# Attention, routing and gated layers on one Trainium2 core: a split, rows, squares, the logits' turn and the constants of attention in other places of the order

## Chip, cores and metric

The kernel runs on one core of a Trainium2 chip, in one launch. The metric is the device time of one execution in microseconds (us). One execution is profiled: its span, from its first to its last instruction, and the waits inside it are read from its trace. TensorE is PE in the rows (PEld its weight loads), VectorE is DVE, ScalarE is ACT, GpSimd is POOL and SyncE is SP.

## The reference

Three stages follow each other. The attention has no sum over a row: a sigmoid stands where a softmax would.

```python
scores = scale * np.matmul(q, k.transpose(0, 1, 3, 2)) - np.log(S)   # 4 x 12 heads, S = 448, width 64
attn = 1.0 / (1.0 + np.exp(-scores))
x = np.matmul(attn, v)                                               # -> 1792 tokens x 768

xn = x / (np.linalg.norm(x, axis=-1, keepdims=True) + 1e-06)         # experts' directions alike: en
logits = xn @ en.T / tau                                             # 8 experts
expert_idx = np.argmax(logits, axis=1)
out[mask] = gate_w[mask, None] * (np.maximum(x[mask] @ w1[e], 0.0) @ w2[e])   # F = 1024

gate = 1.0 / (1.0 + np.exp(-(x @ w_gate)))                           # x: the 1792 x 768 of the experts
return (gate * (x @ w_val)) @ w_out                                  # F = 1536
```

## The kernel before

**Exact products from two parts.** Nearly every matrix product is computed as three: an operand is split into a rounded part `hi` and the rest `lo`, and hi*hi, hi*lo and lo*hi are added in PSUM. For weights, `split_next` takes the next chunk of 128 x 1536 from the list `order`: ACT casts it to `hi` (L213), VectorE subtracts (L214). A parameter `hi_eng` lets VectorE do the cast too. The two parts go into a ring of four buffers, and `take` hands them out in the same order. `split_pair` does the same for queries and keys of a pair of heads, both steps on VectorE (L351, L352).

**Attention.** It handles the heads in pairs, 24 in all, six for each of four sequences, and one turn of the loop `for g in range(2 * ND + 1)` works on one pair, g = 0 to 24. In a turn TensorE computes scores in units of 128 keys (`qk_unit`, L377), ACT applies the sigmoid (L379), and later TensorE multiplies with the values (`av_unit`, L391). All `av` products of the kernel share one PSUM tile of two halves, one for each pair of two. When a pair's last unit is added, VectorE copies its half out as `xT` (L396), and TensorE begins the other pair's next products only after that copy. Two pairs share one unit of left-over keys, which runs as unit 3.

**What is hung into the turns.** The function `attention_hooks(g, pos)` is called three times a turn: pos 0 at its start, pos 1 behind the scores, pos 2 behind the value products. Everything else is written out there by hand, so the place in this function is the place in each engine's order: splits of the next pair, loads, the decoding of 64-bit weights on VectorE (L196, L199, L202), `logits` (L407, TensorE, added up in `lgT` on VectorE, L411 and L413), `logits_turn` (L417, one transpose of `lgT` on TensorE, then a copy, L418), `rows_unit`, and from `G0 = 19` on the first steps of the routing. With the loop's turn counted from G0, `at_` (3, 2), (4, 0) and (4, 2) are the places of the first three weight splits.

**Rows and squares.** `rows_unit(b, c)` turns 112 tokens of a finished sequence from columns to rows: six transposes on TensorE (L431), a copy on ACT (L433), a store to `xd` in memory that GpSimd issues (L434), and `square` on ACT (L423), which adds up the squares for the norm. The four parts of a sequence b have their places at turns `LG[b]`, +1, +2 and +2, all at pos 2, LG = 7, 13, 19. For the last sequence `rows_part` (L446, L448, L449) and `rows_pair` (L461, L464, L465) do it in pieces, and nine of their squares are kept in the list `squares` for later. The row copies share three buffers in SBUF (tag `xr`), so a copy waits until the store that used its buffer three copies before has landed.

**Constants and directions.** `prepare_constants` (L313 to L317 on VectorE, the square of the experts' directions on ACT, L321, its root on GpSimd, L323) and `prepare_directions` (L303 to L330, VectorE) make the normalized directions; `prepare_experts` turns them on TensorE (L334) and copies them to `en` on VectorE (L335).

**Behind attention.** `front(p)` gathers nothing itself: it transposes the gathered tokens of tile p (L839), casts them to `xh` (L844, ACT) and `xl` (L846, VectorE). `h_chunk(0, 0..3)` multiplies tile 0 with the four chunks of its expert's first weights (L990). In between stand the rest of the counting: `count`, `ranks`, `columns`, `first_ids` (L588, with a copy of the numbers to VectorE, L589), then `gather(1)` (L830), which GpSimd issues when these numbers and all stored rows are there. `place_a` to `place_c` work out on VectorE where each token goes, GpSimd multiplies (L595) and TensorE collects the ids (`psid`, L602).

**PSUM.** Beside the tile of `av` three slots of two banks go round: the fourth tile asked for waits until the first was read. A tile is read by ACT or VectorE, so TensorE waits for these engines in the order in which the slots go round.

Of the kernel before, what the change touches and what calls it, by code (L numbers as in the profile page):

```python
# [28 lines left out]
NCH = S // CP  # L29
# [18 lines left out]
NW1 = KD * F1 // CH  # L48
# [57 lines left out]
def routed_kernel(ctx: ExitStack, tc: tile.TileContext, kqP, vP, emb, tau, w1P, w2P, wffP, cst, out):  # L106
# [11 lines left out]
    def slot(name):  # L118
        return psp.tile([P, 2, 512], F32, tag="ps", name=name)
# [67 lines left out]
    def decode_load(k, src, dst):  # L187

        SP.dma_start(src.bitcast(U32), wffP[k].bitcast(U32))
        dec_t[k] = (src.bitcast(U32).rearrange("p (f w) -> p f w", w=2), dst)  # L190
# [19 lines left out]
    def split(raw, pool, name, width=CH, hi_eng=None):  # L210
        hi = pool.tile([P, width], F32R, tag="hi", name=f"hi{name}")[:, : raw.shape[1]]
        lo = pool.tile([P, width], F32R, tag="lo", name=f"lo{name}")[:, : raw.shape[1]]
        (hi_eng.tensor_copy if hi_eng else A.copy)(hi, raw)  # L213
        V.tensor_sub(lo, raw, hi)  # L214
        return hi, lo

    def split_next(ahead=None, hi_eng=None):
        i = done_split[0]
        if i >= len(order):
            return  # L220
        done_split[0] += 1
        parts[i] = split(raws[raw_of[i]], ring, i, hi_eng=hi_eng)
        j = next((j for j in range(i + 1, len(order)) if order[j][:2] == ("gv", 0) and order[j][2] in direct), None)
        if j == i + 1:
            f = order[j][2]
            for step in range(3):
                decode(f, step)
            if f + 2 in direct:
                decode_load(f + 2, stage64[f % 2], raws[raw_of[j + 2]])
        it = order[i]  # L230
        if i not in nxt:
            return
        free = [i]
        if it[0] in ("w1", "w2") and PA <= it[1] < PA + NA:

            free = [i - 1, i] if it[2] % 2 else []
            for z in free:
                (h_small if it[0] == "w1" else y_small)(it[1] - PA, order[z][2], raws[raw_of[z]])
        for z in free:
            if ahead is None:  # L240
                load(nxt[z])
            else:
                ahead.append(nxt[z])
# [3 lines left out]
    def take():  # L247
        i = used[0]
        used[0] += 1
        return parts.pop(i)  # L250
# [80 lines left out]
    def prepare_experts():  # L331
        pe_ = slot("pe_")
        for c in range(KD):
            T.transpose(pe_[:, 0, c * E : (c + 1) * E], emb_sb[:, c * P : (c + 1) * P], ident[:E, :E])  # L334
        V.tensor_copy(en[:, :, :E], pe_[:, 0, : KD * E].rearrange("p (c e) -> p c e", e=E))  # L335
        G.tensor_copy(ie[:, :P], ident)
        G.tensor_copy(ie[:, P:], en[:, KD - 1, :E])
# [3 lines left out]
    ss = cpool.tile([CP, NT], F32, name="ss")  # L341
# [79 lines left out]
    def square(xf, acc, name):  # L421
        junk = ap1.tile([CP, D], BF16, tag="junk", name=f"junk{name}")
        A.activation(junk[:, : xf.shape[1]], xf, AF.Square, accum_out=acc)  # L423

    def rows_unit(b, c):

        t = b * NCH + c
        ps = slot(f"xr{t}")
        pv = ps[:CP].rearrange("p a b -> p (a b)")[:, :D]
        for k in range(NPR):  # L430
            T.transpose(pv[:, k * P : (k + 1) * P], xT[b * NPR + k][:, c * CP : (c + 1) * CP], ident)  # L431
        x = ap2.tile([CP, D], F32, tag="xr", name=f"xr_sb{t}", bufs=3)
        A.copy(x, pv)  # L433
        G.dma_start(xd[t * CP : (t + 1) * CP, :], x)  # L434
        square(x, ss[:, t : t + 1], t)

    squares = []

# [94 lines left out]
    def columns(t0, t1):  # L533
        ts_ = slice(t0, t1)
        n = t1 - t0
        TT(out=bm[:, ts_], in0=bct(iota_h[:CP], n), in1=bc3(bi[:, ts_], P), op=ALU.is_equal)
# [48 lines left out]
    def first_ids(k, nt):  # L585
        ps = slot(f"ps0_{k}")
        for t in range(nt):
            T.matmul(ps[:, 0, 0:1], bm[:, t, :], am1[:, k, t : t + 1], start=(t == 0), stop=(t == nt - 1))  # L588
        V.tensor_copy(idx01[:, k : k + 1], ps[:, 0, 0:1])  # L589
# [278 lines left out]
        load_pair(n)  # L868

    ahead = []  # L870
    later = []
    ND = NP // 2

    LG = [NPR * (b + 1) + 1 for b in range(B - 1)]
    G0 = LG[-1]

    def attention_hooks(g, pos):

        at_ = (g - G0, pos)
        n = g + 1  # L880
        if pos == 0 and n < NP:
            split_pair(n)
        if pos == 1 and g % 2 == 0:
            for n in (g + 4, g + 5):
                if n < NP:
                    load_pair(n)
        if pos == 2 and (g + 1) // 2 < ND and g:
            load_v((g + 1) // 2, 1 - g % 2)
        for k in range(DEC_ATT):
            if (g, pos) == (2 * k + 1, 0):  # L890
                decode_load(DEC_ORDER[k], stage_att[k % 2], rawb[:, 2 + k % 2, :])
            for step, when in enumerate(((2 * k + 2, 1), (2 * k + 2, 2), (2 * k + 3, 1))):
                if (g, pos) == when:
                    decode(DEC_ORDER[k], step)
        if pos == 2 and g >= 3 and g % 2:
            logits([g - 3, g - 2])
        if (g, pos) == (1, 1):
            prepare_constants()
        elif (g, pos) == (1, 2):
            prepare_directions()  # L900
        elif (g, pos) == (2, 1):
            prepare_experts()
        for b in range(B - 1):
            if (g, pos) == (LG[b], 2):
                logits_turn(b)
                if b == B - 2:
                    choose(0, TE)
                    RED(out=ohf, in_=oh[:, :TE].rearrange("p t e -> p e t"), axis=AX.X, op=ALU.add)
                    V.tensor_copy(ohs, ohf)
                    V.tensor_copy(oh4, bct(ohf, NCH))  # L910
            for c in range(NCH):
                if (g - LG[b], pos) == ((0, 2), (1, 2), (2, 2), (2, 2))[c]:
                    rows_unit(b, c)
        if at_ == (1, 1):
            count(0, TE)
        elif at_ == (1, 2):
            fullest()
            expert[0] = SP.value_load(es["tile"], min_val=0, max_val=E - 1)
            ranks(0, TE)
            fullest_ids(0, TE)  # L920
            first_tiles(0, TE)
        elif at_ == (2, 1):
            columns(0, TE // 2)
        elif at_ == (2, 2):
            columns(TE // 2, TE)
        elif at_ == (3, 1):
            first_ids(0, TE)
            gather(0)
        for c, when in enumerate(((2, 1), (2, 2), (3, 1), (3, 2))):
            if at_ == when:  # L930
                load(order.index(("w1", 0, c)))
        if at_ == (4, 1):
            for k in (0, 1):
                load(order.index(("w2", 0, k)))
        for c, when in enumerate(((4, 1), (4, 2), (4, 2), (5, 1))):
            if at_ == when:
                rows_part(c)
        if at_ in ((3, 2), (4, 0), (4, 2)):
            split_next(ahead, hi_eng=V if at_ == (4, 0) else None)

    for g in range(2 * ND + 1):
# [36 lines left out]
    def h_chunk(p, c, between=None, part=None):  # L978
        if c == 0:
            hp_t[p] = slot(f"h{p}")  # L980
        ps = hp_t[p]
        xh, xl = xg_t["T", p]
        hi, lo = part or take()

        passes = ((xh, hi), (xh, lo), (xl, hi))
        for part in (passes[:2], passes[2:]) if c == 0 else (passes,):
            for s in range(3):
                k, half = divmod(3 * c + s, 2)
                for x, w in part:
                    T.matmul(ps[:, half, :], x[:, k * P : (k + 1) * P], w[:, s * 512 : (s + 1) * 512],  # L990
                             start=(k == 0 and x is xh and w is hi), stop=(k == KD - 1 and x is xl))
                if between and s == 1 - c and part[0][0] is xh:
                    between()
        if c == NW1 - 1:
            h = mp.tile([P, F1], F32, tag="h", name=f"hr{p}", bufs=1)
            h_t[p] = h
            relu(p)
# [224 lines left out]
    rows_pair(NPR - 1, SP)  # L1222
    choose(TE, NT)
    later.pop()()
    w1_0 = [take() for _ in range(NW1 - 1)]
    h_chunk(0, 0, lambda: count(TE, NT), part=w1_0[0])
    fullest_ids(TE, NT)
    for f in squares:
# [1 line left out]
    ranks(TE, NT)  # L1230
    first_tiles(TE, NT, (1,))
    columns(TE, NT)
    h_chunk(0, 1, lambda: first_ids(1, NT), part=w1_0[1])
    at.close()
    yTp = ctx.enter_context(tc.tile_pool(name="yT", bufs=1, reuse_waits="tile"))
# [6 lines left out]
    for k in range(2, NW2):  # L1242
        load(order.index(("w2", 0, k)))
    split_next(ahead)
    w1_0.append(take())
    h_chunk(0, 2, part=w1_0[2])
    h_chunk(0, 3, part=w1_0[3])
    place_a()
# [211 lines left out]
```

## Time and profile before

| | |
|---|---|
| median of 3 runs | 1015.85 us (1015.69 to 1016.33) |
| the profiled execution, its own time | 1015.3 us |
| its span | 1013.5 us |
| TensorE busy | 983.5 us, 97% |
| weight loads busy | 812.6 us, 80% |
| VectorE busy | 581.7 us, 57% |
| ACT busy | 485.3 us, 48% |
| GpSimd busy | 104.7 us, 10% |
| memory read, written | 197.46 MB, 31.16 MB |

The median is 0.55 us above the profiled execution, and 1.8 us of that execution's time lie outside of its span. Busy shares are means over stages of different kinds: attention fills about the first 160 us, the first tiles' routing the next 40, then come the experts and the gated layers. A row of a timeline gives the start in the span, the duration, and in brackets how long the engine stood idle before it and which instruction ended that. In the kernel's engines instructions run in the order in which they are written, so an instruction that waits holds up all behind it on its engine.

### The profile page before, as it was taken

The numbers are of one execution on the slowest core, as the hardware profiler recorded it, in microseconds if no ns is written. First come the engines' busy times: TensorE is split into PE (matmuls) and PEld (weight loads), VectorE is DVE, ScalarE is ACT, GpSimd is POOL, SyncE is SP. The second block draws the span as 40 slices with busy tenths as digits, with TensorE's granted clock in tenths as the row PEclk, the third lists the DMA queues.
The fourth block names the chain that finished last, engine by engine and source line by source line (L and its number), as shares of the span: only waits on it lengthen the run. The fifth ranks groups of instructions, "written<-read, shape, count | busy, mean of one in ns | idle before, by whom it ended". The sixth has DMA issues, their size and how long they took to land.

```text
span 1013.5 us, 15157 instructions
## 1 busy us (share of the span) xinstructions
PE 983.5 (97%) x6096; PEld 812.6 (80%) x6096; DVE 581.7 (57%) x652; ACT 485.3 (48%) x528; POOL 104.7 (10%) x103
## 2 busy tenths in 40 slices
PE   8999998989999999999999999999999999999995
PEld 4455454778888888889888899888899888999995
DVE  5867664987887777876588533333333333323551
ACT  5576675467776677776322422333322333223540
POOL 0011002213231221201000001000001000001001
PEclk9999998999999999999999999999999999999998
DMA  8999866374799974692578533322333322324530
GB/s 283 332 337 321 286 212 222 113 263 160 281 362 346 318 286 168 220 326 81 220 230 299 187 125 126 124 94 94 125 125 140 109 94 94 125 94 173 193 103 31
DMA packets 39695, 198.23 MB, mean 196 GB/s; under 512 B 5032, under 2 KB 7096, under 8 KB 37184
## 3 DMA queue, kind: packets, MB, share of 16 engines
q1 hardware_dynamic: 31584, 158.68, 45.5%
q0 software_dynamic: 8032, 38.51, 9.8%
q8 instruction: 49, 0.80, 0.3%
q14 instruction: 30, 0.25, 0.1%
HBM read 197.46 MB, written 31.16 MB: 226 GB/s over the span
## 4 chain that ended last, share of the span: by engine, by line
PE 73%; DMA 2%; issue 1%; DVE 0%; POOLq 0%
PE gv L1208 11%; PE gv L1209 11%; PE gv L1210 11%; PE h L990 7%; PE o L975 6%; PE o L976 6%; PE o L974 6%; PE y L974 3%; PE y L975 3%; PE y L976 3%; PE qh L1079 2%; PE qy L1102 1%; PE hTp L1009 1%; DMA xg<-xd,idx 1%; PE yTp L1194 1%
## 5 line engine op out<-in xcount | busy, mean ns | idle before, releaser
L214 DVE TENSOR_TENSOR lo<-rawb,hi 128x1536 fp32r<-128x1536 f32 x176 | 307.2, 1758 | 295.8 <-ACT hi L213 293.1
L213 ACT CAST hi<-rawb 128x1536 fp32r<-128x1536 f32 x175 | 258.1, 1480 | 240.7 <-PE gv L1209 97.2
L1208 PE MATMUL gv<-yT,hi 128*128 128x512 f32 (+1 forms) x576 | 208.9, 363 | 0.0
L1210 PE MATMUL gv<-yT,lo 128*128 128x512 f32 (+1 forms) x576 | 208.9, 363 | 0.0
L1209 PE MATMUL gv<-yT,hi 128*128 128x512 f32 (+1 forms) x576 | 208.8, 363 | 0.0
L1210 PEld LDWEIGHTS gv<-yT,lo 128*128 128x128 f32 x576 | 108.7, 189 | 16.9
L1208 PEld LDWEIGHTS gv<-yT,hi 128*128 128x128 f32 x576 | 108.7, 189 | 16.7
L1209 PEld LDWEIGHTS gv<-yT,hi 128*128 128x128 f32 x576 | 108.7, 189 | 16.6
L974 PE MATMUL o<-hi,gh 128*128 128x384 f32 x336 | 112.8, 336 | 0.0
L976 PE MATMUL o<-lo,gh 128*128 128x384 f32 x336 | 112.3, 334 | 0.0
L975 PE MATMUL o<-hi,gl 128*128 128x384 f32 x336 | 112.3, 334 | 0.0
L379 ACT ACTIVATE attn<-sc,bias_s 128x896 f32<-128x896 f32 x84 | 78.3, 1005 | 30.4 <-PE sc L377 30.4
L1368 ACT CAST gh<-sg 128x512 fp32r<-128x512 f32 (+1 forms) x48 | 27.2, 567 | 129.8 <-DVE sg L1367 129.8
L391 PE MATMUL av<-attn,v 128*64 128x448 f32 (+1 forms) x384 | 72.9, 558 | 6.1 <-DVE xT L396 6.1
L974 PE MATMUL y<-hi,hh 128*128 128x384 f32 x208 | 72.1, 346 | 0.0
L990 PE MATMUL h<-hi,xh 128*128 128x512 f32 x168 | 68.3, 406 | 3.6 <-PEq L1133 3.5
L975 PE MATMUL y<-hi,hl 128*128 128x384 f32 x208 | 70.1, 337 | 0.0
L976 PE MATMUL y<-lo,hh 128*128 128x384 f32 x208 | 70.0, 336 | 0.0
L990 PE MATMUL h<-lo,xh 128*128 128x512 f32 x168 | 66.3, 395 | 0.1
L975 PEld LDWEIGHTS o<-hi,gl 128*128 128x128 f32 x336 | 63.1, 188 | 0.1
L974 PEld LDWEIGHTS o<-hi,gh 128*128 128x128 f32 x336 | 63.1, 188 | 0.1
L976 PEld LDWEIGHTS o<-lo,gh 128*128 128x128 f32 x336 | 63.1, 188 | 0.0
(304 smaller groups left out, 1178.0 us busy)
## 6 DMA issues: line engine op xcount, KB each, us to landing
rawb<-wd SPq DMA_DIRECT2D x65, 768.0 KB
rawb<-in_w1P SPq DMA_DIRECT2D x52, 768.0 KB
rawb<-in_w2P SPq DMA_DIRECT2D x52, 768.0 KB
rawb<-in_wffP SPq DMA_DIRECT2D x16, 1536.0 KB
wd<-rawb POOLq DMA_DIRECT2D x16, 768.0 KB, 6.7
kq<-in_kqP SPq DMA_DIRECT2D x24, 448.0 KB
xd<-xr_sb POOLq DMA_DIRECT2D x12, 336.0 KB, 7.3
y<-yd SPq DMA_DIRECT2D x10, 384.0 KB
```

The lines of the kernel that those rows point to most:

```text
L213: (hi_eng.tensor_copy if hi_eng else A.copy)(hi, raw)
L214: V.tensor_sub(lo, raw, hi)
L379: A.activation(at_, ps[:, :, :S], AF.Sigmoid, bias=bias_s, scale=1.0 / math.sqrt(HD))
L391: T.matmul(av_t[j * HD : (j + 1) * HD, i % 2, :S], v[rows, j * HD : (j + 1) * HD], at_[rows, j, :], start=(u == first_unit(i)), stop=(u == ...
L974: T.matmul(o, ah[:, ks], bh[:, w], start=(k == 0), stop=False)
L975: T.matmul(o, al[:, ks], bh[:, w], start=False, stop=False)
L976: T.matmul(o, ah[:, ks], bl[:, w], start=False, stop=(k == nk - 1))
L990: T.matmul(ps[:, half, :], x[:, k * P : (k + 1) * P], w[:, s * 512 : (s + 1) * 512], start=(k == 0 and x is xh and w is hi), stop=(k == KD ...
L1208: T.matmul(o, hi[:, a, k, :], yh[:, k, :n], start=(k == 0), stop=False)
L1209: T.matmul(o, hi[:, a, k, :], yl[:, k, :n], start=False, stop=False)
L1210: T.matmul(o, lo[:, a, k, :], yh[:, k, :n], start=False, stop=(k == KD - 1))
L1368: A.copy(gh[:, f, :n], sg[:, :n])
```

## The change

No instruction is added or removed: the engines have as many rows as before, in another order. Five things move. `prepare_constants` goes from the hook (1, 1) to (0, 1) and `prepare_directions` from (1, 2) to (1, 1). In a turn of `LG`, `rows_unit` now comes ahead of `logits_turn`. The squares of a sequence's third and fourth rows (c = 2, 3) are put off to the next pos 1, behind four sigmoids. The third weight split leaves (4, 2), in the last full turn, and comes behind `columns(TE, NT)`, between the first two chunks of tile 0. As its parts are taken later, `take` is called for two chunks first and for two later on.

```diff
-    def rows_unit(b, c):
+    def rows_unit(b, c, put_off=None):
...
-        square(x, ss[:, t : t + 1], t)
+        if put_off is None:
+            square(x, ss[:, t : t + 1], t)
+        else:
+            put_off.append(lambda: square(x, ss[:, t : t + 1], t))
...
-    later = []
+    later, put_off = [], []
...
-        if (g, pos) == (1, 1):
+        if (g, pos) == (0, 1):
             prepare_constants()
-        elif (g, pos) == (1, 2):
+        elif (g, pos) == (1, 1):
             prepare_directions()
         elif (g, pos) == (2, 1):
             prepare_experts()
+        if pos == 1:
+            while put_off:
+                put_off.pop(0)()
         for b in range(B - 1):
+            for c in range(NCH):
+                if (g - LG[b], pos) == ((0, 2), (1, 2), (2, 2), (2, 2))[c]:
+                    rows_unit(b, c, put_off if c > 1 else None)
             if (g, pos) == (LG[b], 2):
                 logits_turn(b)
...
-            for c in range(NCH):
-                if (g - LG[b], pos) == ((0, 2), (1, 2), (2, 2), (2, 2))[c]:
-                    rows_unit(b, c)
...
-        if at_ in ((3, 2), (4, 0), (4, 2)):
+        if at_ in ((3, 2), (4, 0)):
             split_next(ahead, hi_eng=V if at_ == (4, 0) else None)
...
-    w1_0 = [take() for _ in range(NW1 - 1)]
+    w1_0 = [take() for _ in range(NW1 - 2)]
...
     columns(TE, NT)
+    split_next(ahead)
     h_chunk(0, 1, lambda: first_ids(1, NT), part=w1_0[1])
...
     split_next(ahead)
-    w1_0.append(take())
+    w1_0 += [take(), take()]
     h_chunk(0, 2, part=w1_0[2])
```

TensorE at the first logits' turn (g = 7, pos 2; `lp` are the logits, `lg` the turned logits, `xr` the rows). Before:

```order
L407 MATMUL lp_632<-xT_545,en 32x112 x4
L407 MATMUL lp_632<-xT_585,en 32x112 x4
L417 MATMUL lg_642<-cs,lgT_416 112x128
L431 MATMUL xr_645<-cs,xT_310 112x128
L431 MATMUL xr_645<-cs,xT_360 112x128
```

and now:

```order
L407 MATMUL lp_632<-xT_545,en 32x112 x4
L407 MATMUL lp_632<-xT_585,en 32x112 x4
L431 MATMUL xr_642<-cs,xT_310 112x128
L431 MATMUL xr_642<-cs,xT_360 112x128
L431 MATMUL xr_642<-cs,xT_433 112x128
L431 MATMUL xr_642<-cs,xT_473 112x128
L431 MATMUL xr_642<-cs,xT_545 112x128
L431 MATMUL xr_642<-cs,xT_585 112x128
L417 MATMUL lg_654<-cs,lgT_416 112x128
```

The six transposes of the rows have changed places with the one of the logits.

VectorE at the end of attention (the last two copies of `xT` are those of pairs 22 and 23). Before:

```order
L413 TENSOR_TENSOR lgT_1607<-lgT_1607,lp_1760 128x112
L214 TENSOR_TENSOR lo_1791<-rawb,hi_1790 128x1536
L396 COPY xT_1798<-av 128x448
L396 COPY xT_1814<-av 128x448
L413 TENSOR_TENSOR lgT_1607<-lgT_1607,lp_1816 128x112
```

and now:

```order
L413 TENSOR_TENSOR lgT_1607<-lgT_1607,lp_1760 128x112
L396 COPY xT_1794<-av 128x448
L396 COPY xT_1810<-av 128x448
L413 TENSOR_TENSOR lgT_1607<-lgT_1607,lp_1812 128x112
L418 COPY lg<-lg_1836 112x32
```

The `lo` of the third split is gone from here. It stands further on, as the next place shows for its `hi`.

ACT behind attention, now (`junk` are the squares that had been kept, nine in all, of which the last five are shown; before, only the second of the two casts stood here):

```order
L423 ACTIVATE junkp_3_1892,ssp<-xrp_sb 112x128
L423 ACTIVATE junkp_0_1894,ssp<-xrp_sb 112x128
L423 ACTIVATE junkp_1_1896,ssp<-xrp_sb 112x128
L423 ACTIVATE junkp_2_1898,ssp<-xrp_sb 112x128
L423 ACTIVATE junkp_3_1900,ssp<-xrp_sb 112x128
L213 CAST hi_1909<-rawb 128x1536
L213 CAST hi_1961<-rawb 128x1536
L1008 ACTIVATE hr_1983<-h_1859 128x512 x2
```

The cast of the third split (`hi_1909`) now waits behind the nine squares, next to that of the fourth. On VectorE its `lo` stands ahead of the copy of the numbers for `gather(1)`.

## Rows read from the trace of the kernel before

**Rows 1.** Waits of TensorE over the span: us in total, times, longest.

```profile
PE av L391 <- DVE xT L396: 6.1, 2, 4.4
...
PE lg L417 <- DVE lgT L413: 3.1, 3, 1.1
PE sc L377 <- ACT attn L379: 2.0, 3, 0.7
```

**Rows 2.** Page, part 2: busy share of the DMA engines, 40 slices, tenths.

```profile
DMA  8999866374799974692578533322333322324530
```

**Rows 3.** Timeline, VectorE and TensorE, 10 to 23 us: start, us, idle before.

```profile
10.85 0.63 DVE L351 CAST kqhi<-kq 128x896 fp32r<-128x896 f32 x1 [3.29 <-DMA kq<-in_kqP]
...
12.52 0.16 DVE L313 RECIPROCAL tau_sb<-tau_sb 128x1 f32<-128x1 f32 x1
...
14.53 0.14 DVE L303 TENSOR_SCALAR rt<-rt 8x1 f32<-8x1 f32 x1 [1.38 <-POOL rt L323]
...
19.07 2.48 PE L391 MATMUL av<-attn,v 128*64 128x448 f32 x12 [1.65 <-DVE xT L396]
...
20.48 0.20 DVE L335 COPY en<-pe__344 128x48 f32<-128x48 f32 x1
...
22.18 0.37 PE L377 MATMUL sc<-kqhi 64*128 64x448 f32 x2
```

**Rows 4.** Timeline, TensorE and VectorE, around the first and third logits' turn.

```profile
49.62 0.29 PE L417 MATMUL lg<-cs,lgT 128*112 128x128 f32 x1 [1.05 <-DVE lgT L413]
49.75 0.82 PE L431 MATMUL xr<-cs,xT 128*112 128x128 f32 x6
...
130.44 0.62 DVE L396 COPY xT<-av 128x448 f32<-128x448 f32 x1
...
131.54 2.48 PE L391 MATMUL av<-attn,v 128*64 128x448 f32 x12
```

**Rows 5.** Timeline, ACT and TensorE, around the first and third pair of rows.

```profile
67.62 0.47 PE L377 MATMUL sc<-kqhi 64*128 64x448 f32 x2 [0.66 <-ACT attn L379]
...
148.29 1.48 ACT L213 CAST hi<-rawb 128x1536 fp32r<-128x1536 f32 x1
...
150.38 2.80 ACT L379 ACTIVATE attn<-sc,bias_s 128x896 f32<-128x896 f32 x3 [0.60 <-PE sc L377]
...
151.49 0.65 PE L446 MATMUL xr<-cs,xT 128*112 128x128 f32 x4
```

**Rows 6.** Timeline, all engines, from the end of attention to tile 1.

```profile
153.95 0.55 POOL L449 DMA_DIRECT2D xd<-xr_sb  x1 [0.30 <-ACT xr_sb L448]
...
161.99 4.75 PE L391 MATMUL av<-attn,v 128*64 128x448 f32 x12 [4.41 <-DVE xT L396]
...
162.37 0.58 ACT L448 COPY xr_sb<-xr 112x512 f32<-112x512 f32 x1 [2.76 <-DMA xd<-xr_sb]
...
167.99 0.82 PE L839 MATMUL xTp<-cs,xg 128*128 128x128 f32 x6
...
169.85 0.48 PE L990 MATMUL h<-hi,xh 128*128 128x512 f32 x1
...
174.71 1.01 POOL L830 DMA_INDIRECT xg<-xd,idx  x1 [4.89 <-DVE idx L589]
...
174.76 1.47 ACT L213 CAST hi<-rawb 128x1536 fp32r<-128x1536 f32 x1
...
175.80 0.39 PE L990 MATMUL h<-lo,xh 128*128 128x512 f32 x1
...
176.26 1.76 DVE L214 TENSOR_TENSOR lo<-rawb,hi 128x1536 fp32r<-128x1536 f32 x1 [1.83 <-ACT hi L213]
...
180.04 0.82 PE L839 MATMUL xTp<-cs,xg 128*128 128x128 f32 x6
...
191.94 0.55 PE L602 MATMUL psid<-spi,bm 112*128 112x26 f16 x16 [1.10 <-POOL spi L595]
```

**Rows 7.** Windows, same place: length, busy of PE, PEld, DVE, ACT, POOL, clock, DMA.

```profile
162.00:164.00 2.00, 2.00 (x6) 0.76 (x8) 0.00 (x0) 0.58 (x1) 0.52 (x1) 0.50 0.03 12
```

## The prediction

> **What bounds the kernel now.** I read the list of TensorE's waits first, then the timeline around each, then the clock. TensorE is busy 97% of the span, so whatever moves the end is one of its few waits or its clock; VectorE and ACT, busy about half the time, matter only where TensorE waits for them. Three waits of the list lie in the stretch that the change touches [rows 1]: the value products for the copy `xT` (6.1 us in two places), the logits' turn for `lgT` (3.1 in three), the scores for a sigmoid (2.0 in three); 11.2 us together. [...] All later stages follow TensorE's order and shift as a whole, so what TensorE gains up to tile 1 (180 us) I carry to the end. Nothing is added: each gain below is a wait that goes, less the part that something later in line keeps.
>
> **A, constants and directions.** VectorE waited 3.29 us for the keys at the start, until 10.85 [rows 3]. The five constants (L313 to L317) now lie ahead of that wait and fit into it, if their loads are there. The directions then begin where the constants stood, at 12.52 and not at 14.53, 2.0 sooner, and with them the wait of 1.38 for the root from GpSimd is over, since ACT's square of the directions moves forward too. Everything behind on VectorE, the `xT` copy among it, comes 2.0 sooner. TensorE waited 1.65 for that copy before 19.07 [rows 3], so this wait goes whole. What is late next is `en`: its copy ran from 20.48 to 20.68, behind the decoding of weights that come by DMA and do not come sooner, and the score product that needs its PSUM slot, at 22.18 before, would be due at 20.53. I take 0.2 off: A = 1.4. Lower bound 1.1, if the constants' loads land with the keys (five small instructions of some 0.14, 0.16 by the first one's row, then cost 0.7 of the 2.0, and 0.2 stays lost); upper bound 1.65.
>
> **B, the logits' turn.** Three times TensorE stood 1.05 us before the turn, for an addition on VectorE that the change does not move [rows 1, 4]. Six transposes of rows, 0.82 us [rows 4], now run ahead of it. I count 0.75 of them, since the end of a product overlaps the next (the turn's own product runs 0.29, and the next starts 0.13 behind it). So 0.3 of each wait stays, and three times 0.75 = 2.25 goes. The third time something else is late: VectorE has the sequence's choice of experts to do, its `xT` copy ended at 130.44 + 0.62 = 131.06, and TensorE, which began the next value products at 131.54 [rows 4], would now arrive at 130.79. 0.3 is lost there: B = 1.95. Lower bound 1.5 (the third gives nothing), upper bound all 3.15.
>
> **C, the squares.** At the first two places the sigmoid that TensorE waits 0.66 for [rows 5] stands behind two squares. A row copy of 112x512 takes 0.58 on ACT [rows 6]; by that a square of 112x768 is estimated at 0.87, and two put off free 1.7, more than the wait: 1.3 for both. The third time the squares come ahead of the cast `hi` at 148.29 [rows 5]. The cast starts some 0.45 later, and so does the sigmoid behind it, which waited 0.60 for its scores; the wait of 0.67 goes, but the transposes of the last sequence's rows, at 151.49, wait for the slot which that sigmoid reads, and get 0.2 of it. C = 1.5, between 1.2 (the third turns to a loss of 0.1) and 2.0.
>
> **D, the third split.** VectorE's `lo` (1.76 us) and the wait for its `hi` stood ahead of the last `xT` copies. Without them the value products start at 161.99 - 4.41 = 157.6, and without that idle time I expect full clock: 2.48 and not 4.75, another 2.3. TensorE would then be free for tile 0's transposes (167.99 [rows 6]) at about 161.4, 6.6 sooner. But these need the slot which ACT's last row copy reads, and that copy waited until 162.37 for a store that GpSimd issued at 153.95, three copies earlier [rows 6]. Nothing moves the store. The copy ends at 162.95, the transposes start at 163.0, and the first chunk's products (169.85) at 164.9: 5.0 sooner, not 6.6.
>
> What is late next is the split itself. ACT has nine squares and then a cast; that cast began at 174.76 with no idle time before it [rows 6], so now at 169.8. It ends at 171.2 (1.47), VectorE's `lo` (1.76) at 173.0. The third chunk's second product, the first to read `lo`, ran at 175.80 [rows 6] and would be due at 170.8; now it can start at 173.05, 2.75 sooner. Then tile 1: its gather, issued at 174.71, needs a copy of numbers that VectorE now makes behind `lo`, so it goes out at 173.45, 1.25 sooner. Tile 1's transposes ran at 180.04, at most 5.3 behind the gather's issue, so they come at 178.8 at worst (1.25) and at 177.1 at best (3.0). The third chunk allows 2.75. At 191.94 TensorE waited 1.10 for the placing [rows 6], and VectorE's placing chain now comes some 3 us sooner, so up to 1.1 of what tile 1 loses is taken up there: between 1.25 + 1.1 = 2.35 and 2.75 is left, of which I take the upper half: D = 2.6. Lower bound 0 (the gather takes 2 us longer), upper bound 4.6 (the store is no bound).
>
> On that store: it carries 112 x 512 numbers, 224 KB, and its buffer was free 8.4 us behind its issue [rows 6]. [...]
>
> **Sum.** 1.4 + 1.95 + 1.5 + 2.6 = 7.45 us. The profiled execution took 1015.3 (span 1013.5 and 1.8 around it), which gives 1007.85 for one like it; the median is 0.55 above it: 1015.85 - 7.45 = **1008.4**. All lower bounds give 3.8 (1012.0), all upper ones 11.4 (1004.5). The cover for what I cost at nothing: the moved squares and casts lie beside sigmoids or products, as ACT and VectorE wait for TensorE through most of attention; where that cover is gone I counted the loss (third squares, third chunk).
>
> **Rivals.** R1, every wait goes and nothing keeps a part: 11.2 and the clock's 2.3, 13.5 us, 1002.4. For it: all four engines but TensorE have room. Against: the store and the `lo` behind nine squares are plain orders of instructions. 8%.
>
> R2, the last part gives nothing, because cast and `lo` come later than I think or the gather does: 1.4 + 1.95 + 1.5 = 4.85, 1011.0. For it: the gather can only be issued 1.25 sooner. Against: the wait of 1.10 at the placing has room for such a loss. 15%.
>
> R3, the gains are given back to the DMA, or the moves do nothing that shows. Its engines are 80 to 90% busy in most of the first 150 us [rows 2], so an attention that is a few us shorter may wait for weights or keys. Against: none of TensorE's waits above ends with a transfer. I give it a gain under 2, about 1014.5. 7%.
>
> R4, slower: the clock. Before, idle time of 4.41 us was followed by 0.50 [rows 6, 7]. Now there are holes before 163.0 (1.6 us), at the third chunk (2.2) and before tile 1 (about 1), close to each other, and if the clock falls in the first and does not rise between them, the 12.05 us of work from 167.99 to 180.04 take 24.1, the holes vanish in it, and tile 1 comes at 187.1: 7.1 later than before. The sum is then 4.85 - 7.1, a loss of 2.25: 1018.1. It decides from the point where that stretch loses 9.5 us against the forecast. Against: a wait of 1.65 at 19.07 left the products behind it at 2.48 [rows 3]. 4%. [...]
>
> **Chances and range.** The forecast has 66%. The range is that of the bounds, 1004.5 to 1012.0; it holds the forecast and R2, 81%. 0.2%, 2 us, is about what a measurement of this kernel tells from no change: faster by more, forecast, R1 and R2, 89%; within it R3, 7%; slower R4, 4%.
>
> **What would show it.** In the profile after, among TensorE's waits: no `xT` wait of 1.65 at 17 us and none of 4.41 at 157 (A, D); the turns' waits at about 0.3 three times (B); no wait of 0.66 for a sigmoid (C). The twelve products near 157 at 2.48 and the clock full through to 180. In D's place new ones: for a PSUM slot until 163 less what A to C give (about 5), for `hi` and `lo` at the third chunk, for tile 1's tokens. I am wrong if the gather of tile 1 is not issued sooner at all, if the store's landing moves with A to C by less than they give, or if the clock falls anywhere new.

## The result and the profile after

The changed kernel takes 1006.4 us (median of 4 runs, 1005.96 to 1009.09), the kernel before 1016.0 on the same chip: a ratio of 0.9903, 95% interval 0.9888 to 0.9917, so 9.6 us less. The forecast was 1008.4 within 1004.5 to 1012.0, and faster. The profiled execution's span went from 1013.5 to 1004.4 us, 9.1 less.

TensorE's waits over the span of the changed kernel (us in total, times, longest), the answer to [rows 1]:

```profile
PE h L996 <- PEq L1139: 3.0, 1, 3.0
PE y L982 <- DVE lo L214: 1.4, 2, 0.8
PE xTp L842 <- DMA xg<-xd,idx: 1.3, 1, 1.3
PE h L996 <- DVE lo L214: 1.3, 1, 1.3
...
PE xr L449 <- ACT attn L379: 0.9, 1, 0.9
PE lg L417 <- DVE lgT L413: 0.7, 3, 0.3
PE psid L605 <- POOL spi L598: 0.7, 1, 0.7
...
PE sc L377 <- DVE en L335: 0.6, 1, 0.6
PE h L996 <- ACT hi L213: 0.6, 1, 0.6
PE av L391 <- DVE xT L396: 0.3, 2, 0.2
```

The wait for `xT` is down from 6.1 to 0.3 and the one for `lgT` from 3.1 to 0.7; the score products no longer wait for a sigmoid. New ones have come, each behind a part of the change: 0.6 for `en` (A), 0.9 before the last sequence's rows (C), 0.6, 1.3 and 1.3 at the third chunk and tile 1 (D). The wait for `lo` at L982, 0.8 before, has grown by 0.5 near 229 us; in the second execution of the change it is 0.8 again.

The timeline of TensorE at those places (start, duration, in brackets the idle time before), the answer to the rows of [rows 3 to 6] with the same lines:

```profile
21.29 0.47 PE L377 MATMUL sc<-kqhi 64*128 64x448 f32 x2 [0.62 <-DVE en L335]
...
48.84 0.29 PE L417 MATMUL lg<-cs,lgT 128*112 128x128 f32 x1 [0.25 <-DVE lgT L413]
...
147.29 0.65 PE L449 MATMUL xr<-cs,xT 128*112 128x128 f32 x4 [0.93 <-ACT attn L379]
...
153.54 2.48 PE L391 MATMUL av<-attn,v 128*64 128x448 f32 x12 [0.17 <-DVE xT L396]
...
156.77 0.82 PE L842 MATMUL xTp<-cs,xg 128*128 128x128 f32 x6
158.63 0.48 PE L996 MATMUL h<-hi,xh 128*128 128x512 f32 x1
...
165.06 0.50 PE L996 MATMUL h<-hi,xh 128*128 128x512 f32 x1 [0.56 <-ACT hi L213]
...
166.85 0.50 PE L996 MATMUL h<-lo,xh 128*128 128x512 f32 x1 [1.29 <-DVE lo L214]
...
172.31 0.87 PE L842 MATMUL xTp<-cs,xg 128*128 128x128 f32 x6 [1.31 <-DMA xg<-xd,idx]
...
183.26 0.55 PE L605 MATMUL psid<-spi,bm 112*128 112x26 f16 x16 [0.73 <-POOL spi L598]
```

The twelve value products behind the last `xT` wait take 2.48 and not 4.75, and tile 0's transposes start at 156.77 with no idle time before them: no store holds them. ACT, VectorE and GpSimd at the same place:

```profile
155.00 0.59 ACT L451 COPY xr_sb<-xr 112x512 f32<-112x512 f32 x1 [0.95 <-DMA xd<-xr_sb]
...
163.55 2.83 ACT L213 CAST hi<-rawb 128x1536 fp32r<-128x1536 f32 x2
165.04 1.76 DVE L214 TENSOR_TENSOR lo<-rawb,hi 128x1536 fp32r<-128x1536 f32 x1 [2.35 <-ACT hi L213]
...
166.72 0.15 DVE L592 CAST idx<-ps 128x1 int32<-128x1 f32 x1
...
167.14 2.27 POOL L833 DMA_INDIRECT xg<-xd,idx  x1 [8.55 <-DVE idx L592]
```

The row copy waits 0.95 for the store and starts at 155.00, where it waited 2.76 and started at 162.37 [rows 6]. The cast stands behind the squares until 163.55, `lo` behind the cast, the numbers behind `lo`, the gather behind the numbers: the chain that the prediction laid out.

### The profile page after: what moved, and what is told of

It reads as the page before. It is cut to its first block, busy times and chain, and to the rows that moved or that the text cites. A ratio compares the mean times of both kernels' runs of the same rounds, so it can differ in the third digit from the quotient of the medians.

```text
span 1004.4 us, 15151 instructions
## 1 busy us (share of the span) xinstructions
PE 981.1 (98%) x6096; PEld 812.2 (81%) x6096; DVE 581.3 (58%) x652; ACT 486.1 (48%) x528; POOL 105.9 (11%) x103
## 4 chain that ended last, share of the span: by engine, by line
PE 76%; DVE 0%; issue 0%; DMA 0%; POOLq 0%
PE gv L1215 11%; PE gv L1214 11%; PE gv L1216 11%; PE h L996 8%; PE o L982 6%; PE o L980 6%; PE o L981 6%; PE y L980 3%; PE y L982 3%; PE y L981 3%; PE qh L1085 2%; PE qy L1108 1%; PE hTp L1015 1%; PE yTp L1200 1%; PE xTp L842 1%
## 5 line engine op out<-in xcount | busy, mean ns | idle before, releaser
L982 PE MATMUL o<-lo,gh 128*128 128x384 f32 x336 | 112.3, 334 | 0.0
L391 PE MATMUL av<-attn,v 128*64 128x448 f32 (+1 forms) x384 | 70.7, 546 | 0.3 <-DVE xT L396 0.3
L982 PE MATMUL y<-lo,hh 128*128 128x384 f32 x208 | 70.1, 337 | 0.5 <-DVE lo L214 0.5
L982 PEld LDWEIGHTS o<-lo,gh 128*128 128x128 f32 x336 | 63.1, 188 | 0.0
```

The lines of the kernel that those rows point to most:

```text
L391: T.matmul(av_t[j * HD : (j + 1) * HD, i % 2, :S], v[rows, j * HD : (j + 1) * HD], at_[rows, j, :], start=(u == first_unit(i)), stop=(u == ...
L982: T.matmul(o, ah[:, ks], bl[:, w], start=False, stop=(k == nk - 1))
```

## The experiments

The theory after the result: A to C are worth what TensorE's waits say (4.2 us), and D's size hangs on the store of rows, which lands when the weight loads of SyncE ahead of it have drained, not a fixed time behind its issue. The rivals: the store takes 8.4 us whatever else moves, as the sum had it; or D simply adds to the rest. A second question was what D still loses at the third chunk and tile 1.

On the chip of the first four runs the kernel before ranged from 1014.09 to 1018.96 us, and the intervals reach 1.2 to 1.8 us to either side, so the traces decide.

### The change without D (e1_abc)

```diff
-        if at_ in ((3, 2), (4, 0)):
+        if at_ in ((3, 2), (4, 0), (4, 2)):
...
     columns(TE, NT)
-    split_next(ahead)
```

> The change without D: the third split back in its old place, A, B and C kept. By the waits of the changed kernel's trace A to C give 4.25 us (A 0.93, B 2.25, C 1.07), so about 1011.7, with the wait of some 4.4 us for xT and the lower clock back near 158 us. By the prediction's own terms (1.4 + 1.95 + 1.5 = 4.85) 1011.1. If D is what made A to C so large, they give under 3 here, over 1012.9.

Measured: ratio 0.9953 (0.9937 to 0.9970), 4.8 us less than before, between 3.1 and 6.4. The waits:

```profile
PE av L391 <- DVE xT L396: 4.6, 2, 4.4
PE xr L449 <- ACT attn L379: 0.9, 1, 0.9
PE lg L417 <- DVE lgT L413: 0.8, 3, 0.3
```

A to C stand by themselves, and the wait of 4.4 is back, with a granted clock of 0.52 from 157 to 160 us. The `en` wait was missing in this execution: the decoding ahead of `en` waited for its weights until 19.55 us, and until 20.16 in the change. The profiled execution, the slowest of six, also waited 3.6 for a gather of later tokens near 245 us, which no other profile shows.

### D alone, and D alone with two loads later (e2_d_alone, e4_d_alone_late_loads)

D alone is the part of the diff that takes the split from (4, 2) to behind `columns`. The second run also moves two loads:

```diff
-        if at_ == (4, 1):
-            for k in (0, 1):
-                load(order.index(("w2", 0, k)))
...
-    for k in range(2, NW2):
+    for k in range(NW2):
         load(order.index(("w2", 0, k)))
```

> The kernel before with D alone. If the stores of the last rows land when they did before (162.3 us), because the same weight loads lie ahead of them or because a store takes 8.4 us, tile 0's transposes start at 163.0 as the prediction worked out, and the gain is 2.6 to 3.5 us: 1012.4 to 1013.3. If D adds to A to C without regard to them, its gain is 9.6 - 4.25 = 5.35: 1010.6, with the transposes at about 161.

> D alone as in the run above, and SyncE's first two loads of tile 0's second weights (1.5 of the 2.3 MB of weights that it loads near 150 us) issued behind the gather of tile 1 instead. If the stores of rows wait for these loads to drain, they land within 6 us of their issue now, the row copy does not wait, tile 0's transposes start near 161.4 instead of 163.0, and it is about 1.6 us faster than D alone. If a store takes 8.4 us whatever else moves, the two runs are the same within 0.3 us.

Measured: 0.9966 (0.9954 to 0.9978) for D alone, 3.5 us less than before and at most 4.7, so D does not add 5.35 to A to C; 0.9958 (0.9942 to 0.9974) with the loads later, which the times do not tell apart. TensorE in D alone:

```profile
159.74 2.48 PE L391 MATMUL av<-attn,v 128*64 128x448 f32 x12 [0.17 <-DVE xT L396]
163.08 0.87 PE L839 MATMUL xTp<-cs,xg 128*128 128x128 f32 x6
```

and with the loads later:

```profile
157.88 2.48 PE L391 MATMUL av<-attn,v 128*64 128x448 f32 x12 [0.17 <-DVE xT L396]
161.11 0.82 PE L839 MATMUL xTp<-cs,xg 128*128 128x128 f32 x6
```

The first execution was some 1.9 us late by its first logits' turn: behind the wait of 1.65 its value products at 19.36 took 4.04 and not 2.48, at a granted clock of 0.53 from 20 to 22 us. So the starts say little (163.08 meets the expected 163.0 by that delay), and the distance from the value products to the transposes is what to compare: 3.34 and 3.23 us. The store bounds tile 0 by 0.1 in D alone and not at all with the loads later, against the expectation of a wait of 1.6. The first store of the last rows (224 KB, last number: us from issue to landing) shows the reason. Kernel before:

```profile
xd<-xr_sb POOLq DMA_DIRECT2D x1, 224.0 KB, 8.3
```

D alone:

```profile
xd<-xr_sb POOLq DMA_DIRECT2D x1, 224.0 KB, 6.4
```

D alone, two loads later:

```profile
xd<-xr_sb POOLq DMA_DIRECT2D x1, 224.0 KB, 3.2
```

With 1.5 MB of weights out of the way the same store, issued at the same place, takes 3.2 us: the rival of a fixed time has fallen. The queues of the changed kernel agree: from 148.4 to 151.4 us SyncE's loads kept the DMA engines busy at 102% by the profile, and GpSimd's queue moved nothing, though its gather (147.97) and this store (149.81) had been issued.

### The change without C (e3_no_squares)

```diff
-                    rows_unit(b, c, put_off if c > 1 else None)
+                    rows_unit(b, c)
```

> The change without C: the squares back in their places. By the waits of the changed kernel's trace it costs 3 x 0.67 for the sigmoids and gives back the 0.93 of the last sequence's rows: 1.07 us slower than the change, about 1007.4. By the prediction's term (1.5) 1007.9. If the squares do nothing, 1006.4. If putting off the third place's squares is a loss by itself, the wait of 0.93 is gone here and one of 0.67 has come.

Measured: 0.9925 (0.9908 to 0.9943). No run of the change lies beside it on that chip, so the time does not settle 1 us; the waits do:

```profile
PE sc L377 <- ACT attn L379: 2.0, 3, 0.7
PE lg L417 <- DVE lgT L413: 0.8, 3, 0.3
PE xTp L842 <- ACT xr_sb L451: 0.5, 1, 0.5
```

The three waits of 0.67 are back, the one of 0.93 is gone: C is worth 2.0 - 0.93 = 1.1. And here the store does hold tile 0, by 0.5: it took 6.9 us.

### The change again (e5_after_again)

No edit.

> The changed kernel itself, beside the three that follow: its ratio to the kernel before should be 0.9903 within the interval of the first comparison (0.9888 to 0.9917), and its trace should show the same new waits of TensorE: 0.56 and 1.29 at the third chunk, 1.31 before tile 1, 0.73 at the placing, 0.62 for en, 0.93 before the last sequence's rows. If some of these were chance of one execution, they differ by over 0.2 us.

Measured: 0.9902 (0.9886 to 0.9919), the first result again, but in a profiled execution with a span of 1008.5, the longest of its four. The waits of 0.61, 0.91, 0.54, 1.29 and 0.73 are there. The third logits' turn waited 0.86 in place of 0.25, and a later tile waited 1.1. The store took 7.3 us, and TensorE waited 0.90 for the row copy before tile 0. And behind the waits of 0.54 and 1.29 at the third chunk the clock fell (windows: length, busy of PE, PEld, DVE, ACT, POOL, clock, DMA, GB/s):

```profile
166.00:168.00 2.00, 0.50 (x1) 0.19 (x1) 1.50 (x1) 1.84 (x2) 0.00 (x0) 1.00 0.99 412
168.00:170.00 2.00, 1.68 (x6) 1.40 (x7) 2.00 (x4) 0.00 (x0) 1.40 (x1) 0.84 0.07 28
170.00:172.00 2.00, 2.00 (x6) 1.52 (x6) 1.79 (x11) 0.00 (x0) 0.88 (x1) 0.50 0.26 55
```

In the first profile the same stretch, with the same waits, had 1.00 throughout, and the clock fell only later, to 0.50 from 186 to 188 us, behind the waits of 0.73 and 0.83 at the placing. That profile is the exception: of the seven with the two waits at the third chunk, six show a clock of 0.50 to 0.53 behind them. D alone, and `lo` behind the numbers (the next run):

```profile
174.00:176.00 2.00, 2.00 (x7) 1.51 (x6) 1.86 (x7) 0.00 (x0) 1.78 (x1) 0.50 0.00 0
```

```profile
168.00:170.00 2.00, 2.00 (x6) 1.55 (x5) 1.83 (x10) 0.00 (x0) 0.00 (x0) 0.50 0.00 0
```

Where it falls, TensorE reaches tile 1 later and the wait of 1.31 for the tokens is hidden in that: from the product behind the second wait to tile 1's transposes it is 5.46 us in the first profile, wait included, and 5.6 to 5.8 in the six. What the slower rival of the prediction (R4) supposes thus shows in six of the seven profiles, but for a short time: the slow stretch ends within some 4 us and costs 0.1 to 0.4 by tile 1.

### `lo` behind the numbers (e6_lo_behind), both casts ahead of the squares (e7_casts_ahead, e12_casts_again)

`put_lo` collects the subtraction, which then runs behind `first_ids`:

```diff
     columns(TE, NT)
-    split_next(ahead)
-    h_chunk(0, 1, lambda: first_ids(1, NT), part=w1_0[1])
+    los = []
+    split_next(ahead, put_lo=los)
+    h_chunk(0, 1, ids_then_lo, part=w1_0[1])
```

The second edit takes both casts, of the third and fourth split, to the place ahead of the squares:

```diff
+    los = []
+    split_next(ahead, put_lo=los)
+    split_next(ahead, put_lo=los)
     for f in squares:
         f()
...
     columns(TE, NT)
-    split_next(ahead)
-    h_chunk(0, 1, lambda: first_ids(1, NT), part=w1_0[1])
+    h_chunk(0, 1, ids_then_lo, part=w1_0[1])
...
-    split_next(ahead)
     w1_0 += [take(), take()]
```

> The change with the third split's lo behind the copy of the numbers for the gather on VectorE; its cast stays behind the nine squares. If the gather is late only because that copy stands behind lo, it is issued some 3.5 us sooner (near 163.5 instead of 167.1), the wait of 1.31 before tile 1 goes, and the two waits at the third chunk (0.56, 1.29) stay. VectorE's placing then ends 0.7 sooner, so 0.7 of the 1.31 reaches the end: 0.7 us less than the change. If the gather waits for the last stored rows instead, nothing moves.

> The change with the casts of the third and fourth split ahead of the nine squares on ACT and both lo behind the copy of the numbers on VectorE. If the squares are what keeps the third chunk waiting, its waits (0.56, 1.29) and the one before tile 1 (1.31) go: tile 1 is 3.1 us sooner, and 2.4 of it are left at the placing, whose chain on VectorE comes only that much sooner. 2.4 us less than the change. If the later squares hold up the gates or the first relu, a new wait of up to 2 us stands at the placing and it is the same as the change.

> Both casts ahead of the squares, again, on the same chip as the three above: 0.9889 of the kernel before (0.9872 to 0.9905 the first time), TensorE's waits at the third chunk at most 0.2 and before tile 1 at most 0.1. Its first store of rows lands 10.5 or 12.7 us behind SyncE's first load of the group, the two values that the profiles so far show.

Measured: `lo` behind the numbers 0.9903 (0.9886 to 0.9919), the change's own time within the interval. The gather was issued at 163.54 and not 167.14, and the wait of 1.31 went, as expected; the waits at the third chunk stayed, and here too the clock fell to 0.50 (168 to 170 us). Tile 1 came 5.6 us behind the second wait, as it does in the change with that clock, where the wait of 1.31 is hidden anyway: so there was little to gain.

Both casts ahead: 0.9889 (0.9872 to 0.9905), and 0.9882 (0.9866 to 0.9899) the second time, on another set of runs. Beside the change on the same chip the medians are 1005.27 and 1007.57. In the second execution:

```profile
158.28 2.85 ACT L213 CAST hi<-rawb 128x1536 fp32r<-128x1536 f32 x2
...
161.88 0.16 DVE L595 CAST idx<-ps 128x1 int32<-128x1 f32 x1 [0.35 <-PE ps L594]
161.96 3.43 DVE L217 TENSOR_TENSOR lo<-rawb,hi 128x1536 fp32r<-128x1536 f32 x2
162.46 2.15 POOL L836 DMA_INDIRECT xg<-xd,idx  x1 [5.03 <-DVE idx L595]
163.78 0.50 PE L999 MATMUL h<-lo,xh 128*128 128x512 f32 x1 [0.22 <-DVE lo L217]
...
167.95 0.88 PE L845 MATMUL xTp<-cs,xg 128*128 128x128 f32 x6
```

The third chunk waits 0.22 in place of 1.85, tile 1 for nothing, and the clock was 1.00 there in both executions. From the last value products to the placing TensorE needs 26.9 us in both, against 29.7 (and 31.3 in the second execution) in the change. So the squares were what kept the third chunk waiting. The store of the second execution landed 11.2 us behind the first load, neither 10.5 nor 12.7. The intervals of the two ratios still overlap those of the change; that it beats the change rests on the two medians and the waits together.

### All small waits removed (e8_all), and three kernels with the two loads later (e9, e10, e11)

`e8_all` adds three moves in attention to the casts: `prepare_experts` ahead of the decoding, one square later, two logits' turns later. The other three are the change, the casts ahead, and all moves, each with the edit of the loads above.

```diff
+        if (g, pos) == (2, 1):
+            prepare_experts()
         for k in range(DEC_ATT):
...
-                    rows_unit(b, c, put_off if c > 1 else None)
+                    rows_unit(b, c, last_square if (b, c) == (B - 2, 3) else put_off if c > 1 else None)
-            if (g, pos) == (LG[b], 2):
+            if (g, pos) == ((LG[b], 2) if b == B - 2 else (LG[b] + 1, 1)):
...
                 rows_part(c)
+                while last_square:
+                    last_square.pop(0)()
```

> The run above, and three moves in attention: en's copy ahead of the decoding that waits for a transfer (0.62), the fourth rows' square of the third sequence behind the first copy of the last sequence's rows (0.93), and the first two logits' turns one turn later behind four score units (2 x 0.25). If each of the change's small remaining waits is the one the trace names, they go: 2.0 us less than the run above, 4.4 less than the change, 14 less than the kernel before. If the weights' loads or keys then come too late, waits for transfers appear in attention and up to 2 us are given back.

> The changed kernel with SyncE's first two loads of tile 0's second weights issued behind the gather of tile 1. If the stores of rows land when the weight loads ahead of them have drained, they land within 4 us of their issue here (5.1 and 7.3 us in two profiles of the change) and the wait of 0 to 0.9 us before tile 0's transposes is always 0: the change's time less 0 to 0.9 us. If the later loads crowd the gather or the later splits, up to 1 us is lost again at tile 1 or at the placing.

> The kernel with both casts ahead of the squares, and the two loads late. Casts ahead alone took 0.9889 of the kernel before. If only the store's luck separates executions, 0 to 0.9 us less than that: 0.988 to 0.989. If the gather of tile 1 (issued near 163) now shares the DMA with these loads, its tokens come later and 1 us or more is given back before tile 1: 0.990.

> The run with all moves, and the two loads late. There the fourth row copy waited 4.22 us for a store and TensorE 1.98 before tile 0's transposes. If the loads hold the store, both waits go and tile 0 comes 2.0 us sooner than there; with a wait at the branch near 211 us as in the other runs (3 to 4 us, not 7.93) it is 4.4 us less than the change: 0.986 of the kernel before. If the long wait at the branch belongs to coming sooner to it, it stays near 8 us, and the time is 2 us less than all moves without late loads: 0.9885.

Measured: all moves 0.9905 (0.9888 to 0.9921), no gain on the change where 4.4 us were expected. The small waits went (`en`, the rows, two turns), and the last value products ran at 151.06, 2.5 sooner than in the change. Then:

```profile
155.78 0.58 ACT L454 COPY xr_sb<-xr 112x512 f32<-112x512 f32 x1 [4.22 <-DMA xd<-xr_sb]
156.42 0.88 PE L845 MATMUL xTp<-cs,xg 128*128 128x128 f32 x6 [1.98 <-ACT xr_sb L454]
...
218.88 0.59 PE L1001 MATMUL h<-hi,xh 128*128 128x512 f32 x1 [7.93 <-issue]
```

The store was the bound again, as the prediction had it for the change, the clock fell to 0.50 behind that wait (158 to 160 us), and a branch near 211 us cost 7.93 where other runs show 3 to 4.3.

With the loads later the store lands 3.1 to 3.7 us behind its issue in all three and nothing waits for it. But none is faster for it: the change 0.9910 (0.9894 to 0.9927), the casts ahead 0.9898 (0.9882 to 0.9915), all moves 0.9913 (0.9896 to 0.9929), short of both its expectations. The casts ahead with late loads show where it went:

```profile
171.98 0.88 PE L845 MATMUL xTp<-cs,xg 128*128 128x128 f32 x6 [2.94 <-DMA xg<-xd,idx]
```

The gather of tile 1, issued at 163.47, now has four weight loads shortly ahead of it (from 160.04), where two stood there (from 159.02), and lands 8.5 us later, against 5.5 without the move; in all moves it is 8.3, with a wait of 2.74. In these two the delay went from the store to the gather. In the change with late loads it did not: its gather goes out 5 us later and took 5.3. There the store had held at most 0.9, and the profiled execution lost 1.70 to a transfer of values near 75 us; why its time is not lower is not shown further. And in the run of all moves the branch cost 8.78 again.

The store of the first of the last rows, in all profiles:

| kernel | first load of SyncE's group | store issued | landed behind its issue | behind the first load |
|---|---|---|---|---|
| before | 149.56 | 153.95 | 8.3 | 12.7 |
| D alone | 151.58 | 155.96 | 6.4 | 10.8 |
| change without C | 146.81 | 151.20 | 6.9 | 11.3 |
| change without D | 143.73 | 149.17 | 5.3 | 10.7 |
| change | 144.38 | 149.81 | 5.1 | 10.5 |
| change again | 144.76 | 150.16 | 7.3 | 12.7 |
| `lo` behind the numbers | 144.44 | 149.86 | 5.2 | 10.6 |
| casts ahead | 143.63 | 149.05 | 5.1 | 10.5 |
| casts ahead again | 143.22 | 148.65 | 5.8 | 11.2 |
| all moves | 142.88 | 147.42 | 8.3 | 12.8 |
| D alone, two loads later | 149.70 | 154.09 | 3.2 | 7.6 |
| change, two loads later | 146.13 | 151.56 | 3.2 | 8.6 |
| casts ahead, two loads later | 144.31 | 149.74 | 3.1 | 8.5 |
| all moves, two loads later | 143.05 | 147.76 | 3.7 | 8.4 |

The fourth column spreads over 5 us; the last one, with the same loads ahead, lies between 10.5 and 11.3 in seven executions and at 12.7 to 12.8 in three. The kernel before was one of the three. There SyncE's queue still moved single packets (0.02 to 0.04 MB in a microsecond from 159 to 162 us) until about 12 us behind its first load; in the first execution of the change, with 10.5, the last came before 10. Why these packets came so late is open.

## Why the prediction was right, and where it was off

- **A** (1.4 forecast). The wait of 1.65 is gone and 0.62 has come for `en`, behind the decoding that waits for a transfer: a gain of 0.9 to 1.0. The mechanism was the one named; the residue was put at 0.2. It is chance: 0.25 to 0.65 in some runs with A, and missing in others, as the weights land.
- **B** (1.95). Three waits of 1.05 became three of 0.25, and the third place lost 0.15 to `xT` in place of 0.3: 2.25.
- **C** (1.5). Three waits of 0.67 went, and 0.93 came before the last sequence's rows, where 0.2 had been reckoned with: 1.1. The squares held up the sigmoid there by more than was reckoned: it began at 150.38 before [rows 5] and at 146.25 now, 4.1 sooner, where TensorE came 5.1 sooner.
- A to C: 4.2 against 4.85; the last value products were due at 157.58 and now at 153.37. By the same count it is 3.9 to 5.4 in six other profiles with A to C, and 2.5 in the one that lost 1.70 to a transfer.
- **D** (2.6) is the term that was mis-sized: by the placing (191.94 to 183.26) all is 8.7 sooner, so D gave 8.7 - 4.2 = 4.5, nearly its upper bound. The wait for `xT` gave 4.2 and the full clock 2.8 (2.3 forecast, from 4.75 and 2.48 [rows 6, 3]: the slow stretch had reached beyond the twelve products), so tile 0's first chunk came 7.0 sooner, not 5.0. The step that failed is "Nothing moves the store": A to C were to bring it forward by what they give, and its issue moved by 4.1, but its landing by 7.4, from 162.29 to 154.93. It went with the loads (6.4 us behind its issue in D alone, 3.2 there with two of them later), and the kernel before had been profiled in one of the three executions where it landed 12.7 to 12.8 us behind the first of them. The losses behind that came as worked out: 1.85 at the third chunk (2.25 forecast), 1.31 at tile 1, some 0.3 in gaps too short for the list, and 0.95 given back up to the placing (up to 1.1).
- The size of D is partly luck of that execution. Counted in the same way, from the last value products to the placing, D gave 3.9 in D alone, 4.0 there with the loads later, 3.3 without C, and 2.9 in the second execution of the change, where the store bound tile 0 by 0.90 and the clock fell: there the forecast's 2.6 was nearly met. That the total lies inside the range is luck in part too: A and C fell short by 0.4 each, and B and D went over by 0.3 and 1.9.
- The rest of the 9.1, some 0.4, lies behind 185 us, and later stages did not simply shift, as the prediction had it. The 8.7 of the placing had shrunk to 7.3 at the branch (the clock of 0.50 near 187 us) and was 9.5 at the next tile: the wait at the branch was 2.96 in place of 3.54, and the clock, which had fallen to 0.59 behind it before (226 to 230 us), stayed at 1.00. Then 0.5 went to `lo`. In the other executions but two the wait at the branch is 3.2 to 4.3, so that part is chance.
- **Rivals.** Every wait gone (R1): no, five new ones stand in their place. D worth nothing (R2): no, D alone gave 3.5. The gains given back to the DMA (R3): not in the change, but the store took 8.3 us in `e8_all`, issued while SyncE's loads kept the DMA engines at 102% (147.2 to 148.5 us), and the gather 8.5 and 8.3 in two of the three kernels with late loads. The clock (R4): it fell at the third chunk in six of seven profiles, for some 4 us and not for 12, and in the first profile at the placing. So the prediction's sign "if the clock falls anywhere new" came true, at a small price. The argument against R4 does not hold: the wait of 1.65 near 19 us, followed by products of 2.48 before, was followed by products of 4.04 in D alone. And before, the clock had fallen not only behind the wait of 4.41 but also behind the branch (0.59).

## What to carry to other kernels

The store took 5.1 to 8.3 us in these traces behind SyncE's whole group of loads, and 3.1 to 3.7 with two of them later: before taking "issue to landing" as a constant in a sum, look for the loads that were issued shortly ahead of it, and measure from these. Work that is put off should not stand ahead of what TensorE waits for: here two casts ahead of nine squares were worth about as much as B (2.3 us by the medians, 2.25). And a wait that is removed can come back further on: in `e8_all` the last value products ran 2.5 us sooner, and TensorE waited 1.98 for the store; with both casts ahead and the loads later nothing waited for the store, and TensorE waited 2.94 for the gather. So remove waits one at a time and look at what is late next.

## What the runs showed of the hardware that was not expected

- Two waits of TensorE, 0.54 and 1.29 us with 0.5 of work between them, were followed by a granted clock of 0.50 to 0.53 in six profiles and by 1.00 in one. A wait of 1.65 near 19 us was followed by 0.53 in D alone and by 1.00 in the kernel before and in D alone with the loads later. What decides is not shown.
- TensorE's wait at the branch (L1139 in the change, the code for tiles beyond the fixed number) was 3 to 4.3 us in twelve profiles and 7.9 and 8.8 in those of the two kernels with the three moves in attention, which add no product. In the profile's DMA part two 16 KB instruction loads lie in that wait there, and one in the kernel before, the change and the casts ahead. In those two the first weight load behind the branch ran after 5.1 and 4.7 us, and its product only 3.3 and 4.5 later. That the wait is for these loads is not shown, and which of the three moves brings the second load was not tried. In all moves:

```profile
q8 instruction: 2, 0.03, 1.5%
```

and in the change (windows from TensorE's arrival to its next product):

```profile
q8 instruction: 1, 0.02, 1.6%
```
